# A linear-attention block and a gated expert block in one kernel: where the column sums, the copy of x and the last additions are done

## The chip, the cores and the metric

The kernel runs on one core of a Trainium2 chip. The metric is the device time of one execution in microseconds; "span" is the length of the profiled execution on the core, about 1.7 us less than its timed value. Executions of one kernel differ here by up to 4%, so a change of a few tenths of a microsecond does not show in them. A run counts as slow when it is over 1.5% above the fastest of the same kernel.

The engines: TensorE (PE; PEld is its weight load), VectorE (DVE), ScalarE (ACT), GpSimd (POOL) and SyncE (SP), which issues most DMA transfers. In the lines, ps is PSUM, the memory that takes the results of matmuls and is used here in pairs of banks; an eviction is the VectorE or ScalarE instruction that reads such a result, after which the pair can be filled again. A transfer lands when its data have arrived.

## The reference, cut to what matters

x has 2048 rows (16 tiles of 128) and 640 columns.

```python
xn = layernorm(x)
q, k, v = split(xn @ wqkv)                  # 32 heads of 20
pq, pk = phi(q), phi(k)                     # where(t > 0, t + 1, exp(t)) + 1e-6
kv = einsum("bhsd,bhse->bhde", pk, v)
z  = einsum("bhsd->bhd", pk)                # column sums of pk over all 2048 rows
o  = einsum("bhqd,bhde->bhqe", pq, kv) / (einsum("bhqd,bhd->bhq", pq, z) + 1e-6)
A  = o @ wo
r = xn @ w_r ; idx = top 8 of r             # 8 rows go through the expert
y = (silu(xn[idx] @ w_gate) * (xn[idx] @ w_up)) @ w_down * sigmoid(r[idx])
B  = xn with y added to the rows idx
out = x + A + B
```

## The kernel before

Each tile is normalized (`ln_*`), transposed by a DMA (`dma_tr`), multiplied to k and q (`k_mm`, `q_mm`), and xn^T pk is accumulated (`g_mm`), from which kv follows later. z is a running sum on GpSimd. A DRAM scratch row holds xn beside a copy of x: the gather reads both, and the expert's result is added to the x half.

```python
    def ln_b(t):                                   # L173: the normalization
        sc = rss[t]
        nc.vector.tensor_scalar(
            out=xn[:, t, :], in0=x_sb[:, t, :], scalar1=sc[:, 1:2], scalar2=sc[:, 0:1],
            op0=ALU.subtract, op1=ALU.mult)

    def s_add(t):                                  # L288: column sums, step 1
        ... nc.gpsimd.tensor_tensor(out=S_f[:], in0=S_f[:], in1=pk[:, t, :], op=ALU.add)

    for i in range(8):                             # loads beside the loop, 3 or 2 per repeat
        loads.append((scr_x[256 * i : 256 * i + 256, 0], A_x[0, 256 * i : 256 * i + 256, :]))
        ...                                        # and wg, wu chunk i

    for t in range(2, L - 1):                      # L = 15
        k_mm(t); k_act(t); k_r(t); k_dve(t); s_add(t)
        ln_slot(t + 3)                             # ends with ln_b(t+3), dma_tr(t+3)
        ...
        xstore(t)                                  # xn to the scratch
        for _ in range(3 if t % 2 == 0 else 2): ...   # loads
        g_mm(t - 1); q_mm(t); q_act(t); q_dve(t)

    # after the loop
    router_b(); pz_mm(); router_c(); zm_ops(); router_d()   # router_d issues the gather
    q_dve(L); g_mm(L); ...                         # then den, expert, kv, M
    # y_rows: expert rows + x rows -> scatter to the scratch, then reload x_sb from it

    for t in range(T):                             # L800
        (nc.gpsimd if t % 2 else nc.vector).tensor_tensor(out=xn[:, t, :], in0=xn[:, t, :], in1=x_sb[:, t, :], op=ALU.add)
    for t in range(T):
        a = [4, A0, 6, B0][t % 4]                  # four pairs of PSUM banks in turn
        ...                                        # 10 matmuls, L805
        o_t = evk.tile([P, D], BF16, tag=("ek", "rk")[t % 2], name=f"o{t}")   # 4 output tiles
        nc.vector.tensor_tensor(out=two(o_t[:]), in0=ps[:, a : a + 2, 0:HW], in1=two(xn[:, t, :]), op=ALU.add)  # L810
        (nc.sync if t % 2 == 0 else nc.scalar).dma_start(out_v[:, t, :], o_t[:])
```

## Time and profile before

| | before |
|---|---|
| timed runs | 134.3 to 138.5 us, median 137.5 of three; 135.9 once a fourth run was there |
| span of the profiled run | 134.0 us |
| TensorE / VectorE / GpSimd busy | 112.0 / 104.4 / 68.7 us |
| repeats of tiles 2 to 14 | 47.69 us, of which 43.8 are TensorE's own |
| first to last output matmul | 31.1 us, 7.2 of them idle |

A line of a timeline has start, duration, engine, source line, operation, out<-in, shape, count, and in brackets the idle time before it and what ended it. A line of a group has count, busy time, mean ns of one, and the idle time before. The prediction below shows these lines.

### The profile page before, as it was taken

The numbers are of one execution on the slowest core, as the hardware profiler recorded it, in microseconds if no ns is written. First come the engines' busy times: TensorE is split into PE (matmuls) and PEld (weight loads), VectorE is DVE, ScalarE is ACT, GpSimd is POOL, SyncE is SP. The second block draws the span as 40 slices with busy tenths as digits, with TensorE's granted clock in tenths as the row PEclk, the third lists the DMA queues.
The fourth block names the chain that finished last, engine by engine and source line by source line (L and its number), as shares of the span: only waits on it lengthen the run. The fifth ranks groups of instructions, "written<-read, shape, count | busy, mean of one in ns | idle before, by whom it ended". The sixth has DMA issues, their size and how long they took to land.

```text
span 134.0 us, 2915 instructions
## 1 busy us (share of the span) xinstructions
PE 112.0 (84%) x1101; PEld 77.5 (58%) x1110; DVE 104.4 (78%) x222; ACT 59.8 (45%) x90; POOL 68.7 (51%) x91
## 2 busy tenths in 40 slices
PE   6799689996996989998959998988999206999980
PEld 2267457774774767775737734656767103677750
DVE  0856899999999899999545872679888999456560
ACT  3229737666373576775637437788530000000000
POOL 6640367988889688889990030004065995000000
PEclk9999999999999999999999999999999975799997
DMA  3991245699999999999993294000299102423331
GB/s 97 368 329 38 54 85 138 174 290 145 371 239 293 378 161 309 385 264 372 339 318 123 68 381 147 5 0 5 51 350 355 35 0 98 147 98 128 117 125 71
DMA packets 27013, 24.95 MB, mean 186 GB/s; under 512 B 11368, under 2 KB 25712, under 8 KB 27000
## 3 DMA queue, kind: packets, MB, share of 16 engines
q1 hardware_dynamic: 25080, 22.62, 59.7%
q10 hardware_dynamic: 1824, 2.13, 4.4%
q8 instruction: 8, 0.13, 0.4%
q0 software_dynamic: 96, 0.03, 0.1%
q14 instruction: 5, 0.04, 0.1%
HBM read 17.06 MB, written 7.87 MB: 186 GB/s over the span
## 4 chain that ended last, share of the span: by engine, by line
PE 28%; DVE 27%; DMA 26%; issue 10%; ACT 5%; POOL 1%; SPq 1%; DVEq 0%; POOLq 0%
PE ps L805 14%; DMA xnT<-xn 12%; PE ps L215 5%; DVE xn L800 5%; DMA x_sb<-scr 5%; DVE pk L257 4%; DMA wr<-in_B_w_r_dram 4%; DVE pqT L272 4%; DMA rows<-scr,idx_i 3%; DVE xn L173 3%; DVE stats L138 3%; DVE stats L137 3%; DMA scr<-yrow,idx_i 2%; PE ps L227 2%; ACT rb L601 1%
## 5 line engine op out<-in xcount | busy, mean ns | idle before, releaser
L805 PE MATMUL ps<-M_sb,pqT 128*128 128x320 bf16 x160 | 23.9, 314 | 7.2 <-DVE o L810 7.2
L215 PE MATMUL ps<-wk_sb,xnT 128*128 128x320 bf16 (+1 forms) x140 | 21.7, 301 | 6.4 <-DMA xnT<-xn 6.4
L227 PEld LDWEIGHTS <-wq_sb 128*128 128x128 bf16 x400 | 23.6, 98 | 3.7 <-issue 0.2
L227 PE MATMUL ps<-xnT,wq_sb 128*128 128x128 bf16 x400 | 24.9, 219 | 0.1
L805 PEld LDWEIGHTS <-pqT 128*128 128x128 bf16 x160 | 16.2, 102 | 14.8 <-issue 7.7
L151 POOL TENSOR_TENSOR t<-t,half 128x1 bf16<-128x1 bf16 x16 | 15.2, 948 | 13.7 <-DVE t L147 12.6
L215 PEld LDWEIGHTS <-xnT 128*128 128x128 bf16 x140 | 12.8, 98 | 12.6 <-DMA xnT<-xn 8.1
L288 POOL TENSOR_TENSOR S_f<-S_f,pk 128x640 f32<-128x640 f32 x13 | 18.3, 1410 | 1.2 <-DVE pk L257 0.8
L810 DVE TENSOR_TENSOR o<-ps,xn 128x640 bf16<-128x640 f32 x16 | 12.9, 820 | 7.1 <-PE ps L805 7.1
L266 ACT ACTIVATE eq<-ps 128x640 bf16<-128x640 f32 x16 | 11.3, 704 | 14.4 <-PE ps L227 14.4
L272 DVE SCALAR_TENSOR_TENSOR pqT<-eq,rq 128x640 bf16<-128x640 bf16 x16 | 15.0, 937 | 1.5 <-ACT rq L267 1.4
L173 DVE TENSOR_SCALAR xn<-x_sb,sc 128x640 bf16<-128x640 bf16 x16 | 16.0, 999 | 0.1
L279 PE MATMUL ps<-pk,xn 128*128 128x512 bf16 x55 | 15.6, 378 | 0.5
L800 POOL TENSOR_TENSOR xn<-xn,x_sb 128x640 bf16<-128x640 bf16 x8 | 12.4, 1575 | 5.9 <-DMA x_sb<-scr 5.9
L242 ACT ACTIVATE ek<-ps 128x640 bf16<-128x640 f32 x14 | 9.9, 704 | 9.4 <-PE ps L215 6.9
L257 DVE SCALAR_TENSOR_TENSOR pk<-ek,rk 128x640 bf16<-128x640 bf16 x16 | 13.5, 843 | 0.0
L267 ACT ACTIVATE rq<-ps 128x640 bf16<-128x640 f32 x16 | 11.2, 697 | 0.0
L800 DVE TENSOR_TENSOR xn<-xn,x_sb 128x640 bf16<-128x640 bf16 x8 | 10.5, 1374 | 0.6 <-DMA x_sb<-scr 0.6
L243 ACT ACTIVATE rk<-ps 128x640 bf16<-128x640 f32 x14 | 9.8, 699 | 0.0
L137 DVE BATCH_NORM_STATS2 stats<-x_sb 128x6 f32<-128x320 bf16 x16 | 7.7, 482 | 2.4 <-DMA x_sb<-in_A_x_dram 2.4
L601 ACT CAST rb<-ps 128x1024 bf16<-128x1024 f32 x9 | 8.6, 1021 | 0.9 <-PE ps L589 0.9
L279 PEld LDWEIGHTS <-xn 128*128 128x128 bf16 x64 | 6.0, 97 | 4.8
(128 smaller groups left out, 131.7 us busy)
## 6 DMA issues: line engine op xcount, KB each, us to landing
scr<-xn SPq DMA_DIRECT2D x16, 160.0 KB, 3.9
scr<-in_A_x_dram SPq DMA_DIRECT2D x8, 320.0 KB, 4.6
x_sb<-in_A_x_dram SPq DMA_DIRECT2D x6, 320.0 KB, 4.2
wg_sb<-in_B_w_gate_dram SPq DMA_DIRECT2D x5, 384.0 KB, 5.5
wu_sb<-in_B_w_up_dram SPq DMA_DIRECT2D x5, 384.0 KB, 5.3
wd_sb<-in_B_w_down_dram SPq DMA_DIRECT2D x3, 640.0 KB, 5.7
x_sb<-scr SPq DMA_DIRECT2D x3, 640.0 KB, 7.7
out_dram<-o SPq DMA_DIRECT2D x8, 160.0 KB, 1.8
```

Of the source, the lines that this page charges most:

```text
L137: nc.vector.bn_stats(out=stats[:, 0, :], in_=x_sb[:, t, 0:HW])
L151: nc.gpsimd.tensor_tensor(out=t2[:, 1:2], in0=t2[:, 0:1], in1=half[:], op=ALU.pow)
L173: nc.vector.tensor_scalar(out=xn[:, t, :], in0=x_sb[:, t, :], scalar1=sc[:, 1:2], scalar2=sc[:, 0:1], op0=ALU.subtract, op1=ALU.mult,)
L215: nc.tensor.matmul(ps[:, a + b, 0 : HW + b], lhsT=lhs[:, kc, :] if lhs is not None else xnT[:, kc, tsl(t)], rhs=wk_sb[:, kc, b * HW : (b + ...
L227: nc.tensor.matmul(ps[:, a + m // 4, (m % 4) * P : (m % 4 + 1) * P], lhsT=wq_sb[:, kc, m * P : (m + 1) * P], rhs=xnT[:, kc, tsl(t)], start ...
L257: nc.vector.scalar_tensor_tensor(out=two(pk[:, t, :]), in0=e[:], scalar=1.0, in1=r[:], op0=ALU.min, op1=ALU.add)
L272: nc.vector.scalar_tensor_tensor(out=pqT[:, :, tsl(t)], in0=e[:].rearrange("p (k f) -> p k f", k=KC), scalar=1.0, in1=r[:].rearrange("p (k ...
L279: nc.tensor.matmul(ps[:, 4 + c, :], lhsT=xn[:, t, c * P : (c + 1) * P], rhs=pk[:, t, 0:512], start=(t == 0), stop=(t == T - 1),)
L288: nc.gpsimd.tensor_tensor(out=S_f[:], in0=S_f[:], in1=pk[:, t, :], op=ALU.add)
L800: (nc.gpsimd if t % 2 else nc.vector).tensor_tensor(out=xn[:, t, :], in0=xn[:, t, :], in1=x_sb[:, t, :], op=ALU.add)
L805: nc.tensor.matmul(ps[:, a + b, 0:HW], lhsT=pqT[:, kc, tsl(t)], rhs=M_sb[:, kc, b * HW : (b + 1) * HW], start=(kc == 0), stop=(kc == KC - 1),)
L810: nc.vector.tensor_tensor(out=two(o_t[:]), in0=ps[:, a : a + 2, 0:HW], in1=two(xn[:, t, :]), op=ALU.add)
```

## The change

Its intent: take GpSimd out of VectorE's way, take traffic away from the transposes, and let each tile's last addition stand just ahead of its eviction. z becomes matmuls with ones, four side by side in column groups (the partial sums are folded by a second, small fp32 matmul). The scratch holds xn alone; the expert adds to that, and the reload goes to xn. The diff, cut to its core:

```diff
-    scr = tc.dram_tile([S, 2 * D], BF16, name="scr")
+    scr = tc.dram_tile([S, D], BF16, name="scr")
-    nc.scalar.dma_start(wk_sb[:, 0:2, 0:D], wqkv_v[:, 0:2, D : 2 * D])
+    nc.sync.dma_start(wk_sb[:, 0:2, 0:D], wqkv_v[:, 0:2, D : 2 * D])
...                                    # the same for wk_sb[:, 2:5]
-    def s_add(t):                     # and its calls
...
+    ln_rs(2)                          # front: tile 2 is normalized and transposed
     k_act(1, True)                    # ahead of tile 0's k eviction
-    k_r(0, True)
-    ln_rs(2)
-    k_dve(0)
     ln_b(2)
     dma_tr(2)
+    k_r(0, True)
+    k_dve(0)
...
-    for i in range(8):
-        loads.append((scr_x[256 * i : 256 * i + 256, 0], A_x[0, 256 * i : 256 * i + 256, :]))
...                                    # wg chunks, then wu chunks, remain
-        for _ in range(3 if t % 2 == 0 else 2):
+        for _ in range(2 if t % 2 == 0 or t > 10 else 1):
...
+    def z_mm():
+        for t in range(0, T, 2):
+            for q in range(4):
+                h = q % 2
+                nc.tensor.matmul(
+                    ps[32 * q : 32 * q + 32, A1, 0:HW],
+                    lhsT=ones_b[:], rhs=pk[:, t + q // 2, h * HW : (h + 1) * HW],
+                    start=(t == 0), stop=(t == T - 2), tile_position=(0, 32 * q))
+        nc.scalar.copy(zpart[:], ps[:, A1, 0:HW])
     router_b()
+    z_mm()
+    router_c()
+    g_mm(L)
     pz_mm()                           # now 6 fp32 matmuls zpart x zsel
-    router_c()
     zm_ops()
+    q_dve(L)
     router_d()
-    q_dve(L)
-    g_mm(L)
...
-    for t in range(T):
-        (nc.gpsimd if t % 2 else nc.vector).tensor_tensor(out=xn[:, t, :], ...)
     for t in range(T):
         a = [4, A0, 6, B0][t % 4]
+        nc.vector.tensor_tensor(out=xn[:, t, :], in0=xn[:, t, :], in1=x_sb[:, t, :], op=ALU.add)
...                                    # the last tile is evicted and stored in two halves
```

Left out of this cut: g of tile 0 goes between the two q, one more warm-up matmul stands in the front (`warm(3, 256)` for `warm(2, 256)`), and kv groups 4 and 5 are evicted ahead of the last normalization.

More of the change, by code (lines that the diff above doesn't have):

```diff
@@ L68 @@
     evq = ctx.enter_context(tc.tile_pool(name="evq", bufs=2))
-    scr = tc.dram_tile([S, 2 * D], BF16, name="scr")
+    scr = tc.dram_tile([S, D], BF16, name="scr")
     scr_v = scr.rearrange("(t p) d -> p t d", p=P)
-    scr_x = scr.rearrange("s (a d) -> s a d", a=2)[:, 1:2, :]
     def two(ap):
@@ L96 @@
     ones_f = consts.tile([P, P], F32, name="ones_f")
-    ones_b = consts.tile([P, 1], BF16, name="ones_b")
+    ones_b = consts.tile([P, H], BF16, name="ones_b")
     half = consts.tile([P, 1], BF16, name="half")
@@ L103 @@
     kvT = consts.tile([P, NG, 256], BF16, name="kvT")
-    S_f = consts.tile([P, D], F32, name="S_f")
+    zsel = consts.tile([P, 2], F32, name="zsel")
     r_all = consts.tile([P, T], BF16, name="r_all")
@@ L112 @@
     nc.sync.dma_start(x_sb[:, 0, :], x_v[:, 0, :])
-    nc.scalar.dma_start(wk_sb[:, 0:2, 0:D], wqkv_v[:, 0:2, D : 2 * D])
     nc.gpsimd.dma_start(wr5[:], B_w_r.rearrange("(kc p) -> kc p", p=P))
+    nc.sync.dma_start(wk_sb[:, 0:2, 0:D], wqkv_v[:, 0:2, D : 2 * D])
     nc.sync.dma_start(x_sb[:, 1, :], x_v[:, 1, :])
-    nc.scalar.dma_start(wk_sb[:, 2:5, 0:D], wqkv_v[:, 2:5, D : 2 * D])
+    nc.sync.dma_start(wk_sb[:, 2:5, 0:D], wqkv_v[:, 2:5, D : 2 * D])
     nc.sync.dma_start(x_sb[:, 2, :], x_v[:, 2, :])
@@ L178, in xstore @@
     def xstore(t):
-        nc.sync.dma_start(scr_v[:, t, 0:D], xn[:, t, :])
+        nc.sync.dma_start(scr_v[:, t, :], xn[:, t, :])
     def pe_tr(src, n, k0=0, k1=KC):
@@ L282, in g_mm @@
             )
-    def s_add(t):
-        if t == 1:
-            nc.gpsimd.tensor_tensor(out=S_f[:], in0=pk[:, 0, :], in1=pk[:, 1, :], op=ALU.add)
-        elif t > 1:
-            nc.gpsimd.tensor_tensor(out=S_f[:], in0=S_f[:], in1=pk[:, t, :], op=ALU.add)
     nc.gpsimd.memset(ones_f[:], 1.0)
@@ L294 @@
     nc.gpsimd.memset(xsT[:], 0.0)
+    nc.gpsimd.memset(zsel[:], 0.0)
+    for i in range(4):
+        nc.gpsimd.memset(zsel[32 * i : 32 * i + 32, i % 2 : i % 2 + 1], 1.0 / 32.0)
     nc.gpsimd.memset(grep[:], 1.0)
@@ L309 @@
     nc.scalar.copy(wk_sb[:, :, D], bf(6, KC))
-    warm(2, 256)
+    warm(3, 256)
     ln_st(1)
@@ L328 @@
     ln_st(2)
+    ln_ag(2)
     ln_rs(1)
-    ln_ag(2)
+    ln_t2(2)
+    ln_pow(2)
     ln_b(1)
     dma_tr(1)
-    ln_t2(2)
-    ln_pow(2)
     ev_tr("D", 0, 6)
+    ln_rs(2)
     k_act(1, True)
-    k_r(0, True)
-    ln_rs(2)
-    k_dve(0)
     ln_b(2)
     dma_tr(2)
+    k_r(0, True)
+    k_dve(0)
     ln_st(3)
@@ L350 @@
     ln_rs(3)
-    ln_st(4)
     ln_b(3)
     dma_tr(3)
+    nc.sync.dma_start(x_sb[:, 6:8, :], x_v[:, 6:8, :])
+    ln_st(4)
     ln_ag(4)
-    nc.sync.dma_start(x_sb[:, 6:8, :], x_v[:, 6:8, :])
+    ln_t2(4)
+    ln_pow(4)
+    q_dve(0)
+    g_mm(0)
     q_mm(1)
     q_act(1)
-    q_dve(0)
-    ln_t2(4)
-    ln_pow(4)
-    g_mm(0)
-    s_add(1)
     ln_st(5)
@@ L365 @@
     ln_ag(5)
-    q_dve(1)
     ln_b(4)
@@ L370 @@
     ln_pow(5)
+    q_dve(1)
     xstore(0)
@@ L383 @@
     wu_v = B_w_up.rearrange("(kc p) n -> p kc n", p=P)
-    for i in range(8):
-        loads.append((scr_x[256 * i : 256 * i + 256, 0], A_x[0, 256 * i : 256 * i + 256, :]))
-        if i < KC:
-            loads.append((wg_sb[:, i, :], wg_v[:, i, :]))
-            loads.append((wu_sb[:, i, :], wu_v[:, i, :]))
+    for i in range(KC):
+        loads.append((wg_sb[:, i, :], wg_v[:, i, :]))
+    for i in range(KC):
+        loads.append((wu_sb[:, i, :], wu_v[:, i, :]))
     load_it = iter(loads)
@@ L450 @@
         k_dve(t)
-        s_add(t)
         ln_slot(t + 3)
@@ L472 @@
     k_dve(L - 1)
-    s_add(L - 1)
     g_mm(L - 2, (0, 1))
@@ L487 @@
     A1, B1 = A0 + 1, B0 + 1
+    zpart = moe.tile([P, HW], F32, name="zpart")
+    def z_mm():
[5 more added lines that the diff above has]
+                    lhsT=ones_b[:], rhs=pk[:, t + q // 2, h * HW : (h + 1) * HW],
+                    start=(t == 0), stop=(t == T - 2), tile_position=(0, 32 * q),
+                )
+        nc.scalar.copy(zpart[:], ps[:, A1, 0:HW])
     def pz_mm():
-        for m in range(KC):
+        for m, r0, h, c0, w in (
+            (0, 0, 0, 0, P), (1, 0, 0, P, P), (2, 0, 0, 2 * P, 64), (2, 64, 1, 0, 64),
+            (3, 0, 1, 64, P), (4, 0, 1, 64 + P, P),
+        ):
             nc.tensor.matmul(
-                ps[:, A1, m : m + 1], lhsT=S_f[:, m * P : (m + 1) * P], rhs=ones_f[:, 0:1],
-                start=(m == 0), stop=False, skip_group_check=True,
-            )
-        for m in range(KC):
-            nc.tensor.matmul(
-                ps[:, A1, m : m + 1], lhsT=pk[:, L, m * P : (m + 1) * P], rhs=ones_b[:, 0:1],
-                start=False, stop=True, skip_group_check=True,
+                ps[r0 : r0 + w, A0, m : m + 1], lhsT=zpart[:, c0 : c0 + w], rhs=zsel[:, h : h + 1],
+                start=(m == 0 or r0 == 64), stop=True, skip_group_check=True,
             )
@@ L511 @@
     idx_i = moe.tile([C, 1], I32, name="idx_i")
-    rows = moe.tile([C, 2 * D], BF16, name="rows")
+    rows = moe.tile([C, D], BF16, name="rows")
     gate = moe.tile([C, 1], BF16, name="gate")
@@ L568, in zm_ops @@
         zc = moe.tile([P, KC], F32, name="zc")
-        nc.vector.tensor_copy(zc[:], ps[:, A1, 0:KC])
+        nc.vector.tensor_copy(zc[:], ps[:, A0, 0:KC])
         nc.vector.tensor_tensor(
@@ L715, in y_rows @@
                 out=yrow[:, i * QW : (i + 1) * QW], in0=ps[32 * i : 32 * i + C, n, 0:QW],
-                scalar=gatef[:, 0:1], in1=rows[:, D + i * QW : D + (i + 1) * QW],
+                scalar=gatef[:, 0:1], in1=rows[:, i * QW : (i + 1) * QW],
                 op0=ALU.mult, op1=ALU.add,
@@ L720, in y_rows, with reload @@
             out=scr[:, :], out_offset=bass.IndirectOffsetOnAxis(ap=idx_i[:, 0:1], axis=0),
-            in_=yrow[:], in_offset=None, element_offset=D,
+            in_=yrow[:], in_offset=None,
         )
+    def reload():
         for t0, n_ in ((0, 2), (2, 2), (4, 4), (8, 4), (12, 4)):
-            nc.sync.dma_start(x_sb[:, t0 : t0 + n_, :], scr_v[:, t0 : t0 + n_, D : 2 * D])
+            nc.sync.dma_start(xn[:, t0 : t0 + n_, :], scr_v[:, t0 : t0 + n_, :])
     router_a()
@@ L775 @@
     d4_mm(0, T, (4,))
+    reload()
     nc.scalar.copy(GT[:, 0:4, 512:D], ps[:, A0, :].rearrange("p (c f) -> p c f", c=4))
@@ L783 @@
     kv_ev((2, 3), A1)
+    pkv((4, 5), A0)
+    kv_ev((4, 5), A0)
     norm_half(4, 0, "AD")
     norm_half(4, 1, "AD")
-    pkv((4, 5), A0)
-    kv_ev((4, 5), A0)
     M_mm(0, B0)
@@ L797, with out_add @@
     M_ev(4, B0, "D")
-    for t in range(T):
-        (nc.gpsimd if t % 2 else nc.vector).tensor_tensor(out=xn[:, t, :], in0=xn[:, t, :], in1=x_sb[:, t, :], op=ALU.add)
+    def out_add(t, a, o_t, c0, c1, eng):
+        if c0 == 0 and c1 == D:
+            o, p, x = two(o_t[:]), ps[:, a : a + 2, 0:HW], two(xn[:, t, :])
+        else:
+            b = c0 // HW
+            o, p, x = o_t[:, c0:c1], ps[:, a + b, c0 - b * HW : c1 - b * HW], xn[:, t, c0:c1]
+        nc.vector.tensor_tensor(out=o, in0=p, in1=x, op=ALU.add)
+        eng.dma_start(out_v[:, t, c0:c1], o_t[:, c0:c1])
     for t in range(T):
         a = [4, A0, 6, B0][t % 4]
-        for kc in range(KC):
-            for b in range(2):
-                nc.tensor.matmul(
-                    ps[:, a + b, 0:HW], lhsT=pqT[:, kc, tsl(t)], rhs=M_sb[:, kc, b * HW : (b + 1) * HW],
-                    start=(kc == 0), stop=(kc == KC - 1),
-                )
-        o_t = evk.tile([P, D], BF16, tag=("ek", "rk")[t % 2], name=f"o{t}")
-        nc.vector.tensor_tensor(
-            out=two(o_t[:]), in0=ps[:, a : a + 2, 0:HW], in1=two(xn[:, t, :]), op=ALU.add
-        )
-        (nc.sync if t % 2 == 0 else nc.scalar).dma_start(out_v[:, t, :], o_t[:])
+        nc.vector.tensor_tensor(out=xn[:, t, :], in0=xn[:, t, :], in1=x_sb[:, t, :], op=ALU.add)
+        order = [(kc, b) for kc in range(KC) for b in range(2)]
+        if t == L:
+            order = [(kc, b) for b in range(2) for kc in range(KC)]
+        for kc, b in order:
+            nc.tensor.matmul(
+                ps[:, a + b, 0:HW], lhsT=pqT[:, kc, tsl(t)], rhs=M_sb[:, kc, b * HW : (b + 1) * HW],
+                start=(kc == 0), stop=(kc == KC - 1),
+            )
+        o_t = evk.tile([P, D], BF16, tag=("ek", "rk")[t % 2], name=f"o{t}")
+        if t < L:
+            out_add(t, a, o_t, 0, D, nc.sync if t % 2 == 0 else nc.scalar)
+        else:
+            out_add(t, a, o_t, 0, HW, nc.sync)
+            out_add(t, a, o_t, HW, D, nc.scalar)
 _INS = ['A_x', 'A_wqkv', 'A_wo', 'B_x', 'B_w_r', 'B_w_gate', 'B_w_up', 'B_w_down']
```

## The prediction

> **What bounds the kernel now.** I read the page's chain and groups first, then the timeline of TensorE (PE), then VectorE (DVE) and GpSimd (POOL) in one repeat of the loop, then a table of stretches of the tail. Time is lost on PE in two places. The kernel's 16 row tiles go through a loop whose PE work is k (10 matmuls), g (4) and q (25). The timeline of PE, reduced to the k matmuls (start, duration, what, idle before):
> ```profile
> 17.39 1.56 PE L215 MATMUL ps<-wk_sb,xnT 128*128 128x320 bf16 x10 [1.64 <-DMA xnT<-xn]
> 21.04 1.55 PE L215 MATMUL ps<-wk_sb,xnT 128*128 128x320 bf16 x10
> 24.69 1.55 PE L215 MATMUL ps<-wk_sb,xnT 128*128 128x320 bf16 x10
> ...
> 65.08 1.55 PE L215 MATMUL ps<-wk_sb,xnT 128*128 128x320 bf16 x10
> 68.58 1.56 PE L215 MATMUL ps<-wk_sb,xnT 128*128 128x320 bf16 x10 [1.52 <-DMA xnT<-xn]
> ```
> Without a wait a repeat takes 24.69 - 21.04 = 3.65 us: that is what PE needs. From tile 2 to tile 14 it takes 65.08 - 17.39 = 47.69 us, 12 repeats of 3.97; 12 x 3.65 = 43.8. So 3.9 us are waits for transposes, beside 1.64 before tile 2 and 1.52 before tile 15: some 7 us. Why transposes come late shows in one repeat on DVE and POOL:
> ```profile
> 34.21 1.53 DVE L173 TENSOR_SCALAR xn<-x_sb,sc 128x640 bf16<-128x640 bf16 x1
> 38.30 1.53 DVE L173 TENSOR_SCALAR xn<-x_sb,sc 128x640 bf16<-128x640 bf16 x1
> ...
> 34.16 1.40 POOL L288 TENSOR_TENSOR S_f<-S_f,pk 128x640 f32<-128x640 f32 x1
> 38.26 1.40 POOL L288 TENSOR_TENSOR S_f<-S_f,pk 128x640 f32<-128x640 f32 x1
> ```
> The normalization at L173 takes 0.43 us where POOL rests (12.58, 16.29), and 1.53 where POOL's running sum started 0.05 us earlier. It costs DVE 1.1 us per repeat, so its repeat is 38.30 - 34.21 = 4.09 us, longer than PE's; DVE issues the transposes' input, PE catches up with them and waits. The page's issues say what the queue adds: a transpose lands 4.3 us after issue in the median, 2.6 at best and 6.4 at worst.
>
> The tail is the larger loss. A table of PE alone by stretch (busy, granted clock, DMA share, GB/s):
> ```profile
> 98.90:104.60 5.70, 5.67 (x41) 1.00 0.90 311
> 104.60:111.75 7.15, 0.00 (x0) 0.78 0.03 8
> 111.75:115.00 3.25, 3.25 (x13) 0.50 0.47 172
> 115.00:120.00 5.00, 5.00 (x37) 0.95 0.32 118
> ```
> The output matmuls (L805) fill four PSUM pairs, stop for 7.2 us, and run the next 3 us at half clock. The groups name the cause:
> ```profile
> L805 PE MATMUL ps<-M_sb,pqT 128*128 128x320 bf16 x160 | 23.9, 314 | 7.2 <-DVE o L810 7.2
> L800 POOL TENSOR_TENSOR xn<-xn,x_sb 128x640 bf16<-128x640 bf16 x8 | 12.4, 1575 | 5.9 <-DMA x_sb<-scr 5.9
> L800 DVE TENSOR_TENSOR xn<-xn,x_sb 128x640 bf16<-128x640 bf16 x8 | 10.5, 1374 | 0.6 <-DMA x_sb<-scr 0.6
> ```
> All sums x + xn precede the first eviction (L810) in DVE's order, and DVE and POOL take turns: 1.6 us for an add that takes 0.48 alone (the minimum of that line). The eviction starts at 110.89, though tile 0's matmuls ended near 100.3.
>
> **What the Trainium skill says.** "SBUF — State Buffer", section "Who interferes with whom": a VectorE instruction in a two-port mode, or one with two SBUF inputs against a reading GpSimd instruction, and GpSimd take the shared ports in turn for a whole instruction. The trace agrees (0.43 against 1.53; 0.48 against 1.6). "TensorE: Matmul & The Clock Gate", section "What's actually happening": the clock falls to half after an idle window of about 3.4 us. It agrees: 0.50 after the 7.15 us. "TensorE: Matmul & The Clock Gate", section "Part 3: Packing small matmuls — row/col tiling": matmuls of few columns run side by side. It agrees: the 20 gate matmuls of 384 columns took 0.95 us on the chain, 48 ns each, where a 320-column one alone takes about 140. "DMA: Bandwidth & Descriptors", section "Issuing engines are not separate DMA queues": transfers issued from several engines share the same 16 DMA engines; I expect the removed copies to give their time to the transposes.
>
> **The change part by part.**
> 1. Sums of pk leave POOL (14 adds, 1.4 us each). DVE's repeat should fall from 4.09 to about 3.0 (4.09 - 1.1), below PE's 3.65: PE sets the pace.
> 2. The copies of x in DRAM go: 8 x 320 KB, and 3 or 2 loads per repeat become 2 or 1. The queue moves 12.8 MB or so in the loop, of which 2.6 vanish. Each transpose is issued about 5 us into its repeat and needed 6 us later, so 4 us landing is enough. Parts 1 and 2 together: the 3.9 us and the 1.5 before tile 15, **-5.4 us**.
> 3. The front: tile 2's normalization moves ahead of tile 0's k evictions on DVE, at about 11.4 instead of 12.58; its transpose then lands around 15.5 rather than 17.39, and g of tile 0 moves between the two q, so PE has work until 15.7. All of the 1.64 less a small wait at tile 3 or 4, whose inputs do not come as much earlier: **-1.5 us**. The k weights on the first queue, ahead of x2 and wq, may land earlier; I give it nothing.
> 4. The router and z. Removed from PE: 10 fp32 and 5 bf16 matmuls, from 75.00 to 76.35, 1.35 us on the chain. Added: 32 matmuls of 320 columns, four side by side, 8 x about 0.14 = 1.1 us; a copy of half a bank pair by ScalarE, about 0.4, under g of tile 15; 6 fp32 matmuls, 6 x 0.12 (1.21/10) = 0.7. PE +0.5. zm now waits for these, and tile 15's q comes before the gather's index, so the gather is issued some 2 us later (80.2 against 78.04, on before's clock). It took 4.65 us while the down weights were loading; the scatter, alone, took 2.84. Landing 83.3 against 82.69: **+0.6 us** in all, carried to the reload.
> 5. kv eviction of groups 4 and 5 before the last normalization: takes away a 0.29 us wait, **-0.3 us**.
> 6. Tail: the reload goes to xn after the scatter (95.2 + 0.6), and xn is free by then (its last reader, d4, ends at 92.8). DVE does add, then eviction, tile by tile: 0.4 + 0.75 = 1.15 us against PE's 1.36 (evictions at 116.52 and 130.11 lie ten tiles apart). The first chunk landed 3.1 us after issue, so near 99, before the first eviction at 101. PE should never stop: 16 x 1.36 = 21.8 us from 99 against 130.03 - 98.96 = 31.1 before: **-9.3 us**. The last tile's split eviction halves 0.82: **-0.4 us**.
> Sum: -5.4 - 1.5 + 0.6 - 0.3 - 9.3 - 0.4 = -16.3 us. The span falls from 134.0 to 117.7. A timed run was 1.7 us above its span (135.7), giving 119.4; against the median 137.52 the same difference gives 121.2. I take **120.4 us**.
>
> **Rivals.** (a) The transposes stay late, because landing time is the transposes' own or the weight loads press as before, now packed into a faster loop. For: the queue was at nine tenths nearly throughout the loop, and two normal repeats carry a wait over 1.2 us even though POOL's sum costs only 0.44 per repeat beyond PE. Against: a fifth of the bytes go. It would return 3 to 4 us: 124. (b) DVE becomes the bound in the tail: adds and evictions at 1.15 are near 1.36, and if the add doesn't run at 0.4 while transfers write beside it (say 0.8), DVE's 1.55 sets 16 tiles: +3, 123.5. (c) The last reload chunks hold DVE, which now waits in order: chunk 4 to 7 landed 6.4 us after the first issue, so 102.9 here; DVE wants tile 4 near 105. Against it, then; if it failed by 2 us, 122.4 and no colder clock. (d) The gather takes 4.65 us again: +1.4, 121.8. (e) Only one of the two large parts counts, as the tail might already wait for the reload: no, PE was idle after the data had landed (DMA share 0.03 from 104.6).
>
> **Range and chances.** The runs of before lie 4 us apart, so I allow about +4 for one rival and -3 for a before that was itself slow: 117 to 125. Even all of (a) and (b) together stay near 127, so faster is nearly certain: 0.98, within 2% 0.01, slower 0.01.
>
> **What would show it.** k matmuls 3.65 us apart with no wait named after the transposes; the normalization at 0.43 to 0.6; tile 2's k matmuls near 15.7; the gathered rows landing some 14.7 us after tile 15's k matmuls begin (82.69 - 68.58 = 14.1 before, + 0.6); output matmuls without a gap, clock 1.00, adds near 0.4. I am wrong if DVE shows full in the loop, if waits for transposes stay over 2 us, or if PE idles over 1 us in the tail.

## The result, and the profile after

The changed kernel took 122.71 us in the median (122.23 to 123.78, 4 runs) against 135.9 (134.12 to 138.51, 4 runs). The ratio of the fast runs is 0.9155, with a 95% interval of 0.905 to 0.926. Ratios are the mean time of one kernel's fast runs over that of the other's of the same rounds, so not quite the ratio of the medians. A later series of the same kernel gave 122.0 (120.31 to 122.3, 6 runs) and a ratio of 0.9003. The time lies within the predicted range, 2.3 us above the predicted value.

The k matmuls of the changed kernel, from the timeline of TensorE (tile 3 has two lines; tiles 4 to 9 and 11 to 13 are left out):

```profile
14.24 1.55 PE L214 MATMUL ps<-wk_sb,xnT 128*128 128x320 bf16 x10
17.88 0.30 PE L214 MATMUL ps<-wk_sb,xnT 128*128 128x320 bf16 x1
19.12 1.41 PE L214 MATMUL ps<-wk_sb,xnT 128*128 128x321 bf16 x9 [0.94 <-DVE r_all L252]
...
45.32 1.56 PE L214 MATMUL ps<-wk_sb,xnT 128*128 128x320 bf16 x10 [0.68 <-DMA xnT<-xn]
...
59.90 1.55 PE L214 MATMUL ps<-wk_sb,xnT 128*128 128x320 bf16 x10
62.64 1.56 PE L214 MATMUL ps<-wk_sb,xnT 128*128 128x320 bf16 x10 [0.76 <-DMA xnT<-xn]
```

Tiles lie 3.64 us apart wherever nothing is waited for. Two waits for transposes are left (tiles 10 and 15), and a new one, in the middle of tile 3's matmuls, for VectorE. The normalization, on VectorE's timeline, is back to its undisturbed length:

```profile
31.04 0.45 DVE L172 TENSOR_SCALAR xn<-x_sb,sc 128x640 bf16<-128x640 bf16 x1
34.69 0.45 DVE L172 TENSOR_SCALAR xn<-x_sb,sc 128x640 bf16<-128x640 bf16 x1
```

The output matmuls, from the table of stretches of TensorE (busy, count, granted clock, DMA share, GB/s), no longer stop and no longer meet a slow clock:

```profile
94.11:100.00 5.89, 5.89 (x45) 1.00 0.97 328
100.00:105.00 5.00, 5.00 (x39) 1.00 0.42 154
105.00:110.00 5.00, 5.00 (x39) 1.00 0.35 128
```

But VectorE fell behind at tile 4 and never caught up (its timeline; L817 is the addition, L812 the eviction, the last line the two halves of tile 15):

```profile
99.79 0.82 DVE L812 TENSOR_TENSOR o<-ps,xn 128x640 bf16<-128x640 f32 x1
100.53 0.48 DVE L817 TENSOR_TENSOR xn<-xn,x_sb 128x640 bf16<-128x640 bf16 x1
102.64 0.82 DVE L812 TENSOR_TENSOR o<-ps,xn 128x640 bf16<-128x640 f32 x1 [1.63 <-DMA out_dram<-o]
103.39 0.48 DVE L817 TENSOR_TENSOR xn<-xn,x_sb 128x640 bf16<-128x640 bf16 x1
103.96 0.82 DVE L812 TENSOR_TENSOR o<-ps,xn 128x640 bf16<-128x640 f32 x1
...
117.09 0.89 DVE L812 TENSOR_TENSOR o<-ps,xn 128x320 bf16<-128x320 f32 x2
```

The whole way, cut where both traces have the same event (us from the span's start):

| event | before | after | section shorter by | predicted |
|---|---|---|---|---|
| tile 2's k matmuls begin | 17.39 | 14.24 | 3.15 | 1.5 |
| tile 14's k matmuls begin | 65.08 | 59.90 | 2.03 | 3.9 |
| tile 15's k matmuls begin | 68.58 | 62.64 | 0.76 | 1.5 |
| gathered rows reach TensorE | 82.74 | 78.07 | -1.27 | -0.6 |
| first output matmul | 98.96 | 94.12 | 0.17 | 0.3 |
| last output matmul ends | 130.01 | 116.03 | 9.14 | 9.3 |
| end of span | 134.0 | 120.8 | -0.78 | 0.4 |
| sum | | | 13.2 | 16.3 |

So 9.1 of the 13.2 us come from the output matmuls alone. The shortfall of 3.1 us has three main parts: the loop (2.6 us together with tile 15's wait), the stretch with z and the gather (0.7), and the end (1.2); 0.3 are spread over the rest, and the front gave 1.65 more than I said (2.6 + 0.7 + 1.2 + 0.3 - 1.65 = 3.1). Part of this varies from run to run: a second trace of the changed kernel (11) takes 61.45 - 14.23 = 47.22 us from tile 2 to tile 15, where this one takes 62.64 - 14.24 = 48.40.

### The profile page after: what moved, and what is told of

The parts are those of the page before. It is cut to its first block, busy times and chain, and to the rows that moved or that the text cites. A ratio compares the mean times of both kernels' runs of the same rounds, so it can differ in the third digit from the quotient of the medians.

```text
span 120.8 us, 2944 instructions
## 1 busy us (share of the span) xinstructions
PE 109.2 (90%) x1130; PEld 77.1 (64%) x1140; DVE 91.8 (76%) x231; ACT 60.2 (50%) x91; POOL 38.0 (31%) x74
## 5 line engine op out<-in xcount | busy, mean ns | idle before, releaser
L822 PE MATMUL ps<-M_sb,pqT 128*128 128x320 bf16 x160 | 21.9, 299 | 0.0
L822 PEld LDWEIGHTS <-pqT 128*128 128x128 bf16 x160 | 15.6, 98 | 6.3 <-issue 0.3
L265 ACT ACTIVATE eq<-ps 128x640 bf16<-128x640 f32 x16 | 11.3, 704 | 14.8 <-PE ps L226 14.8
L812 DVE TENSOR_TENSOR o<-ps,xn 128x640 bf16<-128x640 f32 (+1 forms) x17 | 13.3, 785 | 3.3 <-DMA out_dram<-o 1.6
L271 DVE SCALAR_TENSOR_TENSOR pqT<-eq,rq 128x640 bf16<-128x640 bf16 x16 | 13.1, 821 | 2.0 <-ACT rq L266 2.0
L136 DVE BATCH_NORM_STATS2 stats<-x_sb 128x6 f32<-128x320 bf16 x16 | 7.8, 488 | 3.0 <-DMA x_sb<-in_A_x_dram 3.0
L252 DVE CAST r_all<-ps 128x1 bf16<-128x1 f32 x14 | 2.2, 160 | 7.4 <-ACT rk L242 7.4
L389 POOL TENSOR_SCALAR_AFFINE_SELECT grep<-grep 32x640 bf16<-32x640 bf16 x8 | 7.6, 946 | 0.5
L817 DVE TENSOR_TENSOR xn<-xn,x_sb 128x640 bf16<-128x640 bf16 x16 | 7.7, 481 | 0.0
L137 DVE BATCH_NORM_STATS2 stats<-x_sb 128x6 f32<-128x320 bf16 x16 | 7.6, 475 | 0.0
```

Source lines behind the costliest of these rows:

```text
L265: nc.scalar.activation(e[:], src, AF.Exp)
L271: nc.vector.scalar_tensor_tensor(out=pqT[:, :, tsl(t)], in0=e[:].rearrange("p (k f) -> p k f", k=KC), scalar=1.0, in1=r[:].rearrange("p (k ...
L812: nc.vector.tensor_tensor(out=o, in0=p, in1=x, op=ALU.add)
L822: nc.tensor.matmul(ps[:, a + b, 0:HW], lhsT=pqT[:, kc, tsl(t)], rhs=M_sb[:, kc, b * HW : (b + 1) * HW], start=(kc == 0), stop=(kc == KC - 1),)
```

## The experiments

My theory of the whole: GpSimd's sums made VectorE's repeat longer than TensorE's and so the transposes late; the additions ahead of all evictions made the gap in the tail. The main rivals: that the DMA queue made the transposes late, and that contention rather than order made the gap. The second group of runs asks after the shortfall. Some profiled runs were slow (the sum on GpSimd, the tail alone, the additions first, eight output tiles, the k weights on ScalarE); from these I read which wait stands where. Where an amount is read from one of them all the same, it is a stretch of one trace, and weaker than a difference of timed fast runs. The measure for the variants of the changed kernel are its own ten timed runs, 120.3 to 123.8 us.

### 1. The sum on GpSimd put back (pool_sum)

```diff
     k_dve(t)
+    s_add(t)          # S_f on GpSimd; nobody reads it
     ln_slot(t + 3)
```

> The changed kernel with the running sum of pk put back on GpSimd (its result is not used, the output stays right). Theory P (the shared ports set the loop of the kernel before): the normalization on VectorE goes from 0.45 to about 1.5 us in the loop, VectorE's repeat to 4.09 us above TensorE's 3.65; tile 2 to tile 14 takes 47.5 to 49 us instead of 45.66, and waits for transposes come back; total +2 to +4 us. Theory Q (the DMA queue set it): the normalization is longer all the same, but the k matmuls stay near 3.65 apart; total within +0.8 us.

Measured: 128.18 us (125.77 to 129.96), all four above every run of the changed kernel; ratio to before 0.9347. The timelines of VectorE and of TensorE:

```profile
29.16 1.53 DVE L173 TENSOR_SCALAR xn<-x_sb,sc 128x640 bf16<-128x640 bf16 x1
33.25 1.53 DVE L173 TENSOR_SCALAR xn<-x_sb,sc 128x640 bf16<-128x640 bf16 x1
37.35 1.53 DVE L173 TENSOR_SCALAR xn<-x_sb,sc 128x640 bf16<-128x640 bf16 x1
...
35.11 0.30 PE L215 MATMUL ps<-wk_sb,xnT 128*128 128x320 bf16 x1
35.70 1.41 PE L215 MATMUL ps<-wk_sb,xnT 128*128 128x321 bf16 x9 [0.29 <-DVE r_all L253]
```

The normalization is at 1.53 us again and VectorE's repeat at 33.25 - 29.16 = 4.09, exactly as before the change. So the sum alone takes the loop's gain back, and more: from tile 2 to tile 15 it takes 68.19 - 14.69 = 53.50 us, where the kernel before took 51.19. What TensorE then waits for differs from my expectation: at five tiles for VectorE's copy of the router's column, which reads the bank that the second k matmul writes (2.7 us together), and at tile 15 for the transpose (2.98). The transposes land in 2.9 us in the median, sooner than in the changed kernel (3.3), so the sum does not slow the queue; only tile 15's, issued at 61.7 after two weight loads, is used no less than 6.5 us later.

### 2. The copies of x put back (dram_copy)

```diff
+    scr2 = tc.dram_tile([S, D], BF16, name="scr2")
+    for i in range(8):
+        loads.append((scr2[256 * i : 256 * i + 256, :], A_x[0, 256 * i : 256 * i + 256, :]))
         # wg, wu chunk i between them
-        for _ in range(2 if t % 2 == 0 or t > 10 else 1):
+        for _ in range(3 if t % 2 == 0 else 2):
```

> The changed kernel with the eight 320 KB copies of x inside DRAM put back (into a scratch that nobody reads) and the loads at the old pace of 3 or 2 per repeat. Theory Q (the DMA queue makes transposes late): transposes land in 4.3 us median instead of 3.3, waits for them add 2 to 4 us between tile 2 and tile 15, total +2 to +4 us. Theory P (only VectorE's longer repeat mattered, since without it the transposes are issued earlier): landing times rise as well, but the waits grow by under 1 us; total within +1 us.

Measured: 124.96 us (124.35 to 126.27), ratio to before 0.9214. All four runs lie above the ten of the changed kernel, 2.3 us above its first series in the median; by the ratios it is 0.6% above the first series, with overlapping intervals, and 2.3% above the second. Transposes land in 5.2 us in the median instead of 3.3. From tile 2 to tile 15 the trace takes 65.68 - 15.93 = 49.75 us against 62.64 - 14.24 = 48.40, so 1.35 us more, or 2.5 more than the 47.22 of the second trace; the profiled run's late start of tile 2 is explained under 9. Traffic matters, but less than GpSimd's sum, which took that stretch to 53.5 us. So the two act by different ways: the sum lengthens VectorE's repeat, the copies lengthen the landing. Neither of the two theories was right alone: I had written 2 to 4 us for the one and under 1 for the other.

### 3. The tail alone, on the kernel before (tail_only)

```diff
-    for t in range(T):
-        (nc.gpsimd if t % 2 else nc.vector).tensor_tensor(out=xn[:, t, :], ...)
     for t in range(T):
         a = [4, A0, 6, B0][t % 4]
+        nc.vector.tensor_tensor(out=xn[:, t, :], in0=xn[:, t, :], in1=x_sb[:, t, :], op=ALU.add)
```

> The kernel before with one edit: the add of x to a tile moves from the block ahead of all output matmuls (half of it on GpSimd) to just before that tile's eviction, all on VectorE. Theory: the tail's gain does not need the rest of the change: no gap of 7.2 us in the output matmuls, 22 us instead of 31.1 for them, total 126 to 128. Rival: the reload sets the tail once the adds are out of the way, TensorE still idles 2 us or more there, total 129 or above.

Measured: 126.03 us (125.3 to 127.18) against 136.57 (134.6 to 137.7) of the kernel before in the same rounds, ratio 0.929. The timeline of TensorE shows the 160 output matmuls in one piece:

```profile
98.42 21.91 PE L804 MATMUL ps<-M_sb,pqT 128*128 128x320 bf16 x160
```

Moving sixteen additions gives most of the whole gain, and needs nothing else of the change.

### 4. The additions ahead of all evictions, on VectorE alone (adds_first)

```diff
+    for t in range(T):
+        nc.vector.tensor_tensor(out=xn[:, t, :], in0=xn[:, t, :], in1=x_sb[:, t, :], op=ALU.add)
     for t in range(T):
         a = [4, A0, 6, B0][t % 4]
-        nc.vector.tensor_tensor(out=xn[:, t, :], in0=xn[:, t, :], in1=x_sb[:, t, :], op=ALU.add)
```

> The changed kernel with its 16 adds moved ahead of all evictions, but on VectorE alone, so nothing contends for ports. If the order of VectorE's queue made the gap: 16 x 0.48 = 7.7 us of adds stand ahead of the first eviction and wait for the last reload chunk (about 100 us), so the first eviction starts near 103 instead of 95.7, TensorE idles 3 to 4 us after four tiles, total +3 to +5 us. If only the contention of VectorE and GpSimd made it: no gap over 1 us, total within +1 us.

Measured: 127.64 us (126.79 to 129.77), 5 us above the changed kernel. VectorE's and TensorE's timelines:

```profile
99.86 5.07 DVE L807 TENSOR_TENSOR xn<-xn,x_sb 128x640 bf16<-128x640 bf16 x12 [1.69 <-DMA xn<-scr]
104.85 3.01 DVE L815 TENSOR_TENSOR o<-ps,xn 128x640 bf16<-128x640 f32 x4
...
105.72 4.69 PE L824 MATMUL ps<-M_sb,pqT 128*128 128x320 bf16 x17 [4.47 <-DVE o L815]
```

The adds run without contention, and TensorE still stops for 4.47 us; its clock in the 4.28 us after that is 0.50 in the table of stretches. (1.69 us of VectorE's time there is a wait for the reload, which with this order stands ahead of every eviction too.) So the order, with the reload that it puts in front, makes a gap without any contention, by this trace the greater part of that of the kernel before (7.18 us). The split is an estimate from two kernels (the reload is issued 3.6 us ahead of the first output matmul here and 3.8 there); additions tile by tile with half of them on GpSimd, which would show contention alone, were not run.

### 5. Eight output tiles (o_bufs)

```diff
-        o_t = evk.tile([P, D], BF16, tag=("ek", "rk")[t % 2], name=f"o{t}")
+        o_t = (evk, evq)[t // 2 % 2].tile([P, D], BF16, tag=("ek", "rk", "eq", "rq")[t % 4], name=f"o{t}")
```

> The changed kernel with eight output tiles in place of four (two more pools' buffers used in turn). Theory: VectorE's wait of 1.63 us at tile 4 is for the store of tile 0, which stands behind the reload in the same queue, and it pushes the last eviction from about 116.5 to 118; with eight tiles there is no such wait, the last eviction ends 1 to 1.5 us earlier, total -1 to -1.5 us. Rival: VectorE's own 1.31 us per tile against 1.36 of TensorE sets the end; then the wait goes but the end moves by under 0.4 us.

Measured: 120.77 us (120.32 to 122.83), ratio to before 0.892. The wait at tile 4 is gone, and from tile 5 on VectorE's evictions lie 1.36 us apart, TensorE's pace, where they had lain 1.31 apart, its own. VectorE's timeline at tiles 4 and 5:

```profile
102.50 0.82 DVE L812 TENSOR_TENSOR o<-ps,xn 128x640 bf16<-128x640 f32 x1
103.24 0.48 DVE L817 TENSOR_TENSOR xn<-xn,x_sb 128x640 bf16<-128x640 bf16 x1
103.86 0.82 DVE L812 TENSOR_TENSOR o<-ps,xn 128x640 bf16<-128x640 f32 x1
```

From the first output matmul to the end of the last eviction the trace takes 118.29 - 95.50 = 22.79 us against 117.98 - 94.12 = 23.86: 1.07 us less, as the theory had it. The timed runs overlap with the changed kernel's, so the amount rests on the trace.

### 6. The gather before z (gather_first)

```diff
     router_c()
+    router_d()
     g_mm(L)
     pz_mm()
     zm_ops()
     q_dve(L)
-    router_d()
```

> The changed kernel with the gather's index computed on VectorE before z instead of after it and after tile 15's q. The gather is issued near 71.3 instead of 74.75, beside the loads of the down weights. Theory: it lands by 76 and TensorE's 0.65 us wait for the gathered rows is gone, total -0.5 to -0.7 us. Rival: it takes over 4.65 us beside those loads, or moves z later, and nothing is gained (within 0.2 us).

Measured: 122.1 us (121.31 to 123.88); too close to tell by time. In the trace the gather is issued at 71.66, 8.9 us after tile 15's k matmuls instead of 12.1, and the rows reach TensorE without a wait, although the gather, now beside the loads of the down weights, takes 5.4 us to land instead of 3.3:

```profile
77.36 0.27 PE L677 MATMUL ps<-ident,rows 8*128 8x8 bf16 x5
93.41 21.91 PE L822 MATMUL ps<-M_sb,pqT 128*128 128x320 bf16 x160
```

From tile 15's k matmuls to the first output matmul it takes 93.41 - 62.75 = 30.66 us against 31.48: 0.8 less.

### 7. Tile 1's q behind the router's copy (kr_first)

```diff
     ln_pow(5)
-    q_dve(1)
 ...
         k_r(t)
+        if t == 2:
+            q_dve(1)
         k_dve(t)
```

> The changed kernel with q of tile 1 on VectorE moved behind the router's column copy of tile 2. Theory: the gap of 1.1 us in the k matmuls of tile 3 (17.88 to 19.12) is the wait for that copy, which reads the PSUM bank that the second matmul writes; the copy comes 0.7 us earlier, so tile 3's gap shrinks by 0.7 us and the total by 0.5 to 0.7. Rival: the wait is for tile 3's transpose; then nothing moves.

Measured: 122.47 us (121.17 to 124.16), which tells nothing by itself. The k matmuls of tiles 3 and 4 in TensorE's timeline:

```profile
17.99 1.83 PE L214 MATMUL ps<-wk_sb,xnT 128*128 128x320 bf16 x10
22.13 1.55 PE L214 MATMUL ps<-wk_sb,xnT 128*128 128x320 bf16 x10
```

They start 4.14 us apart instead of 22.62 - 17.88 = 4.74. So the new wait of tile 3 was for that copy, and 0.6 us of it goes. The rival, that the transpose was late, would not have moved it.

### 8. z in bf16 (z_bf16)

```diff
-    zsel = consts.tile([P, 2], F32, name="zsel")
+    zsel = consts.tile([P, 2], BF16, name="zsel")
-    zpart = moe.tile([P, HW], F32, name="zpart")
+    zpart = moe.tile([P, HW], BF16, name="zpart")
```

> The changed kernel with the partial z and its selector in bf16 instead of fp32 (a little less exact, within tolerance I expect). It measures the term that I mis-sized: 6 fp32 matmuls show as 12 passes, 1.25 us of TensorE. Theory: 6 bf16 ones take about 0.3, so the stretch from the router's matmul to c4 shrinks by 0.8 to 0.9 us, the gather is issued earlier by as much, total -0.8 us. Rival: the chain there runs over VectorE's wait for z and the gather, and the total moves by under 0.3.

Measured: 121.1 us (120.7 to 121.47), and the result is still correct. The matmuls in question, the first line from the changed kernel's timeline, and with them the rows' arrival:

```profile
71.07 1.25 PE L499 MATMUL ps<-zsel,zpart 128*128 128x1 f32 x12
78.07 0.28 PE L677 MATMUL ps<-ident,rows 8*128 8x8 bf16 x5 [0.65 <-DMA rows<-scr,idx_i]
```

and from the timeline of the variant:

```profile
69.21 0.45 PE L499 MATMUL ps<-zsel,zpart 128*128 128x1 bf16 x6
76.31 0.28 PE L677 MATMUL ps<-ident,rows 8*128 8x8 bf16 x5 [1.55 <-DMA rows<-scr,idx_i]
```

Six fp32 matmuls are twelve passes and 1.25 us, six bf16 ones 0.45. But the 0.8 us only lengthens the wait for the gathered rows, from 0.65 to 1.55: those reach TensorE 76.31 - 60.78 = 15.53 us after tile 15's k matmuls, as before (15.43). The gather is issued 0.8 us earlier (11.3 us after those matmuls instead of 12.1), but lands 4.2 us after its issue instead of 3.3. This is my rival. That the timed runs are 1 us lower in the median all the same I cannot lay to the edit: this trace shows an early front (13.93) and almost no wait at tile 15 (0.15), neither of which it touches.

### 9. The k weights issued by ScalarE again (wk_act)

```diff
-    nc.sync.dma_start(wk_sb[:, 0:2, 0:D], ...)      # and [:, 2:5]
+    nc.scalar.dma_start(wk_sb[:, 0:2, 0:D], ...)
```

> The changed kernel with the two loads of the k weights issued by ScalarE again, as before the change, so that they do not stand in one queue with x. Theory: on one queue the weights land later (about 7.5 us instead of 7.0) and TensorE waits 0.5 to 1.8 us for them in tile 0's k matmuls, which also lets its clock stay at half in some runs; issued by ScalarE that wait goes, tile 2's k matmuls start at 13.5 to 14.5 and spread less, total -0.3 to -1.5 us. Rival: the first tile of x then lands 0.5 us later (3.6 instead of 3.1) and takes it back: within 0.3 us.

Measured: 122.99 us (120.73 to 123.9): no gain that the runs show, a miss for my theory, and the spread is no smaller. Four of the six runs were slow; the ratio of the fast ones, 0.8965, cannot be told from 0.9003 of the changed kernel's second series. TensorE's wait for the weights (0.76 us in the changed kernel) is gone, but its first k matmul starts at 7.32 instead of 6.12, and the first tile of x is at VectorE at 3.58 instead of 3.13. What the front depends on more than on either is seen by comparing two kernels with the same front, the kernel before and the tail alone. TensorE's timeline of the kernel before:

```profile
7.00 1.81 PE L215 MATMUL ps<-wk_sb,cT 128*128 128x320 bf16 x6
8.60 0.74 PE L183 MATMUL ps<-ident,c 128*128 128x128 bf16 x5
9.14 0.96 PE L215 MATMUL ps<-wk_sb,cT 128*128 128x321 bf16 x4
10.22 1.55 PE L215 MATMUL ps<-wk_sb,cT 128*128 128x320 bf16 x10
```

and of the tail alone:

```profile
6.98 0.98 PE L215 MATMUL ps<-wk_sb,cT 128*128 128x320 bf16 x6
7.79 0.44 PE L183 MATMUL ps<-ident,c 128*128 128x128 bf16 x5
8.07 0.71 PE L215 MATMUL ps<-wk_sb,cT 128*128 128x321 bf16 x4
8.90 1.55 PE L215 MATMUL ps<-wk_sb,cT 128*128 128x320 bf16 x10
```

The same instructions run at half pace in one and at full pace in the other, and tile 2's k matmuls follow at 17.39 or 15.97. The changed kernel's front is no different: three of its variants (the copies, the additions first, eight output tiles) begin tile 2 at 15.9 to 16.2, with a granted clock of 0.55 to 0.65 from 8.5 to 12 us, and the others with the k weights on SyncE at 13.9 to 14.7, with 1.00. This trace of the k weights on ScalarE has the half pace too (15.95). In it, as in the kernel before, the record of the granted clock still reads 1.00, so there the clock is inferred from the doubled time of the same matmuls. By that reading, 1.4 us of the front's 3.15 belong to the clock that the profiled run of the kernel before happened to get; like for like it is 15.97 - 14.24 = 1.73, next to the predicted 1.5. It is probably also one source of the spread of the timed runs.

### 10. One load per repeat (fewer_loads)

```diff
-        for _ in range(2 if t % 2 == 0 or t > 10 else 1):
+        for _ in range(2 if t == 2 else 1):
```

> The changed kernel with one load per repeat after the first, so that the last expert weights are loaded after the loop. Theory: the wait before tile 15's k matmuls (0.7 to 1.5 us) comes from loads queued ahead of its transpose, so it falls below 0.3 us; total -0.5 to -1.2 us. Rival: the transpose is simply issued too late by VectorE, and the wait stays; or the late loads delay the gather, and the wait before the gathered rows grows by more than is won.

Measured: 122.33 us (121.51 to 123.44), no gain that the runs show. From the timeline of TensorE:

```profile
60.95 1.55 PE L214 MATMUL ps<-wk_sb,xnT 128*128 128x320 bf16 x10
77.45 0.28 PE L677 MATMUL ps<-ident,rows 8*128 8x8 bf16 x5 [1.73 <-DMA rows<-scr,idx_i]
```

Tile 15's k matmuls start without a wait, 60.95 - 59.13 = 1.82 us after tile 14's instead of 2.74. But that wait differs between runs of the same instructions: the second trace of the changed kernel (11) has 61.45 - 59.48 = 1.97, the trace with eight output tiles a wait of 1.42. So one trace does not show that the loads were its cause. The rows then come 77.45 - 60.95 = 16.5 us later instead of 15.4, with TensorE waiting 1.73 us for them: the loads moved to where the gather runs, as the second half of the rival has it, and the timed runs gain nothing.

### 11 and 12. The changed kernel once more, and the edits together (after_again, combined)

The combination has the edits of 5 to 8 and one load less before tile 15 (`2 if t % 2 == 0 else 1`).

> The changed kernel unchanged, as the measure for the next one on the same chip: 121.5 to 124 us; tile 2's k matmuls start anywhere from 14 to 16 us, as they did in runs of the same instructions.

> The changed kernel with four edits tried alone before (eight output tiles; the gather's index before z; q of tile 1 behind the router's copy; z in bf16) and one load less before tile 15's transpose. Theory: with the gather off TensorE's chain, z in bf16 and the load count pay too, which alone only lengthened the wait for the gathered rows: -0.6 (tile 3), -0.5 (tile 15), -1.4 (z and gather together), -1.1 (end) = -3.6 us, so 118.5 to 120 us. Rival: the gather beside the loads lands late and TensorE waits for it again by 1 us or more; then 120 to 121.

Measured on one chip: 122.0 us (120.31 to 122.3) and 118.6 us (118.0 to 119.0), six runs each; ratios to before 0.9003 and 0.8771. Not one run of the two overlaps. The combination is 3.4 us faster in the median where 3.6 were expected. From the timeline of TensorE of the combination:

```profile
75.62 0.28 PE L678 MATMUL ps<-ident,rows 8*128 8x8 bf16 x5 [0.52 <-DMA rows<-scr,idx_i]
91.67 21.91 PE L823 MATMUL ps<-M_sb,pqT 128*128 128x320 bf16 x160
```

The two traces differ by 119.6 - 117.3 = 2.3 us (this pair of profiled runs lies closer than the medians). Cut at the same events as above: 0.35 more up to tile 2, 0.52 less from there to tile 14 (tile 3's wait), 0.16 less to tile 15, 0.92 less to the gathered rows (75.62 - 61.12 = 14.50 against 76.87 - 61.45 = 15.42), nothing up to the end of the output matmuls, and 1.05 less after them (3.72 against 4.77). Here my expectation had a miss inside: I gave z and the gather together 1.4 us. The gather alone had already brought that stretch to 77.36 - 62.75 = 14.61; z in bf16 adds 0.1, and a wait of 0.52 us for the rows is back. The gather is issued 8.9 us after tile 15's k matmuls and takes 5.5 us to land, beside the loads of the down weights. This version beats both kernels.

## Why the prediction was right, and where its terms were off

**The tail, -9.3.** Right: 9.14. The order of the additions, their contention and the half clock after the idle time were read off the kernel before, and the tail alone shows them to be independent of the rest. Of the two causes the order seems the greater: without contention 4.47 us of idle time stand against 7.18 (4); the reload, for which VectorE waits 1.69 us in that order, is part of them.

**The loop, -5.4 with tile 15's wait.** The mechanism is shown by putting the sum back; its size was 2.8 us (51.19 - 48.40; by the second trace of the changed kernel 4.0). The step that failed is "PE sets the pace": it took no new wait into account. Three were there: tile 3's k matmuls wait for VectorE's copy of the router's column (1.1 us; the change's own order of the front put tile 1's q ahead of it, and moving that gives 0.6 back), tile 10's for a transpose (about 0.8), tile 15's likewise (0.76 left of 1.52, though its second trace has hardly any). "4 us landing is enough" was right as arithmetic, but the transposes of tiles 10 and 15, each issued after two weight loads, landed later: tile 10's, the longest, took 6.0 us, even though the median fell from 4.3 to 3.3. That the loads held them up is not shown (10). This is rival (a), at about half of the size that I gave it (0.84 + 0.76 = 1.6 us against 3 to 4).

**The front, -1.5.** 1.73 like for like; the other 1.4 of the measured 3.15 were, by the pace of the matmuls, the clock, and so luck for the number. I had read the slow k matmuls at 7.00 of the kernel before as its normal pace.

**The router and z, +0.6.** It was +1.27. The mis-sized term is the 6 fp32 matmuls: I divided 1.21 us by the ten passes that the profile lists and took 0.12 for each matmul, but those were five matmuls of two passes each (my "10 fp32" were passes): 1.25 us instead of 0.7. By the bf16 run, TensorE's own work is not what counts there, though: the gather was issued 12.1 us after tile 15's k matmuls (I had put it at 80.2 - 68.58 = 11.6) and was used 3.3 us later (I had allowed 3.1; the 4.65 of rival (d) did not come), and z delays that issue, as VectorE takes the index up after z and tile 15's q. Taking the gather first removes the wait.

**The end, -0.4.** It was +0.78. The step that failed is "DVE does add, then eviction, tile by tile: 0.4 + 0.75 = 1.15": it is 1.31 (the add 0.57 from start to start, the eviction 0.74; I had read 0.48 as the add's least time myself and then reckoned with 0.4), too near to TensorE's 1.36 to make up for anything; and there was something, a wait of 1.63 us for one of four output tiles, whose store was issued at 96.60 while the reload was running. Whether the order in SyncE's queue or the load of the DMA engines held it is not separated: a store from ScalarE's queue, at 100.6, took 3.1 us too, against 1.8 in the median. I looked for the reload as VectorE's wait (rival c) and not as that of the stores. Eight tiles give 1.07 us back.

**The range.** It allowed four us for a rival; what came was 3.1 us of span: three small ones at once, and the lucky front taken off. That the timed runs of the kernel before turned out at 135.9 rather than 137.5 makes the gain in per cent smaller than I expected.

Not settled: why the transposes of tiles 10 and 15 are late in some runs and not in others of the same loop. Six variants with the same loads show no wait at tile 10, and the waits at tile 15 lie between none and 1.5 us; neither follows the edits. Some of the shortfall in the loop is therefore chance.

## What to carry to other kernels

Put a tile's last addition next to its eviction rather than all of them in front: an in-order engine that has sixteen operations ahead of the first eviction stops TensorE as soon as the four PSUM pairs are full, and the clock falls on top of it. Before moving a sum to an idle engine, look at whom it locks out: 1.4 us on GpSimd cost VectorE 1.1 us in each repeat. Before shortening TensorE's own work, find the transfer that runs beside it: 0.8 us less of z only made the wait for the gathered rows 0.9 us longer, while issuing the gather earlier took the wait away.

## What the Trainium skill lacked or had wrong

- "TensorE: Matmul & The Clock Gate", section "What's actually happening": it says that the window over which the clock follows the load is free-running, and the runs fit that: the same front ran at half or full pace from run to run, tile 2 starting at 17.39 us in the kernel before or 15.97 in the tail alone, and at 15.9 to 16.2 or 13.9 to 14.7 in the changed one. It calls the ramp's penalty under 1% of a typical span; here two runs of the same front already differ by 1.4 of 134.0 us, a little over. In the kernel before the record of the granted clock was 1.00 from 5 to 12 us while six k matmuls took 1.81 us instead of 0.98; the same page's warning about such records, in "Seeing it yourself", is borne out.
- "DMA: Bandwidth & Descriptors", section "Issuing engines are not separate DMA queues": it says that issuing from several engines only saves the issue time. It lacks that this can delay another transfer: with the k weights issued by ScalarE the first tile of x was at VectorE at 3.58 to 3.63 us (three traces), from one queue at 3.01 to 3.21 (eleven).
- The pages speak of passes and rates of fp32 matmuls, but I found none with the time of a short one: here one shows as two records in the profile, and six with one moving column took 1.25 us in fp32 and 0.45 in bf16.
- Nor did I find one with a figure for a store issued after a large reload in one queue: an output store of 160 KB lands in 1.8 us in the median, and tile 0's, issued at 96.60 after 2.6 MB of reload, freed its tile only by 102.6.
